# A fused attention and feed-forward kernel whose engine programs are written without a block

## The chip, the cores and the metric

The kernel runs on one core of a Trainium2 chip. The metric is the device time of one execution in microseconds (us); lower is better. Three executions of the kernel before gave 151.01, 150.97 and 151.39 us, a median of 151.01.

A core has five engines that run programs of their own: TensorE (PE, matrix products), VectorE (DVE), ScalarE (ACT), GpSimd (POOL) and SyncE (SP, which here issues nearly all transfers). They meet only through semaphores, counters that one engine or transfer raises and another waits for.

## The reference

The input x has 2048 tokens of 448 columns. It is normalised, and two branches are added to it: linear attention with 16 heads of 28 columns and softmax feature maps, and a feed-forward layer of width 1792 with the Mish activation.

```python
xn = _layernorm(x, axis=-1)
return x + _A_ref(xn, A_wqkv, A_w_phi, A_wo) + _B_ref(xn, B_w1, B_b1, B_w2)

# A: qkv = xn @ wqkv;  pq = q @ w_phi, pk = k @ w_phi (per head)
phi_q = concatenate([softmax(pq), softmax(-pq)]);  phi_k likewise
kv = einsum("bhsf,bhsd->bhfd", phi_k, v);  z = sum over s of phi_k
o = (phi_q @ kv) / (phi_q @ z + 1e-6)
A = o @ wo
# B: h = xn @ w1 + b1;  sp = log(1 + exp(h)), written stably
B = (h * tanh(sp)) @ w2
```

## The kernel before

The 2048 tokens are cut into 16 tiles of 128 (two tiles make a unit u, eight units). Loads of x and of the weights go out on SyncE's queue. VectorE, ScalarE and GpSimd normalise the tiles; the result is transposed and stays in on-chip memory. TensorE then works through keys, values and queries of all units (the helper at line 423 records most of these matmuls), the feed-forward layer's first product (line 423 as well, with the activation at line 699), the sums over tokens (line 649), the attention output (line 722), its product with wo (line 845) and the feed-forward layer's second product (line 828). The last two add up in the same accumulators. VectorE adds x (line 793) and SyncE stores two tiles at a time (line 859). The last tile, `LAST` = 15, is finished in two pieces: 384 columns, stored from ScalarE's queue, and 64 columns (lines 807 to 814), stored from SyncE's queue (both at line 856).

The order of the work is written out by hand: `ORDER` is a list of step names, and `run_order` calls them one by one. A step calls `op` or `dma` of the class `Program`, which only notes an instruction with its engine and what it reads and writes. `resolve` then works out which instructions must wait for which and gives them semaphores; each DMA has a semaphore of its own. Nothing reaches an engine until `emit(name, eng)` goes through one engine's list and writes its waits (line 131) and instructions in order.

After the last step one more instruction is noted, at line 928: an empty one on SyncE that reads every stored tile, and so waits for the landing of each store of the result:

```python
op("SP", lambda e: e.nop(), r=[("dram", t) for t in range(NT)] + [("draml", LAST)])
```

Then `resolve` runs and the five lists are emitted inside `with nc.Block() as block:` (line 931), each in a function of its own. When the `with` ends, the block is closed: every engine drains, and they meet at a barrier, in which GpSimd gathers a count from each engine and then lets all go. In the profile these instructions carry line 931. A similar meeting at the start of the program carries line 964, where the program object is made; it is not part of the kernel's function.

Of the kernel before, what the change touches and what calls it, by code (L numbers as in the profile page):

```python
# [5 lines left out]
ACT = mybir.ActivationFunctionType  # L6
# [132 lines left out]
def bass_parallel_sum__linear_kernel_hedgehog__dense_activation_mish__prompt_kernel(  # L139
    nc, A_x, A_wqkv, A_w_phi, A_wo, B_x, B_w1, B_b1, B_w2, out  # L140
):
    es = ExitStack()
    with es:
        _kernel(es, nc, A_x, A_wqkv, A_w_phi, A_wo, B_w1, B_b1, B_w2, out)
# [26 lines left out]
def _kernel(es, nc, A_x, A_wqkv, A_w_phi, A_wo, B_w1, B_b1, B_w2, out):  # L171
# [87 lines left out]
    pg = Program(nc, es)  # L259
# [668 lines left out]
    op("SP", lambda e: e.nop(), r=[("dram", t) for t in range(NT)] + [("draml", LAST)])  # L928

    pg.resolve()  # L930
    with nc.Block() as block:
        @block.sync
        def _(e):
            pg.emit("SP", e)

        @block.gpsimd
        def _(e):
            pg.emit("POOL", e)

        @block.tensor  # L940
        def _(e):
            pg.emit("PE", e)

        @block.scalar
        def _(e):
            pg.emit("ACT", e)

        @block.vector
        def _(e):
            pg.emit("DVE", e)  # L950


# [26 lines left out]
```

## Time and profile before

| | |
|---|---|
| median of three runs | 151.01 us |
| span of the profiled execution, first to last instruction | 148.7 us, 3864 instructions |
| median less span | 2.3 us |
| TensorE busy | 144.0 us, 97% of the span |
| VectorE, ScalarE, GpSimd busy | 102.7, 74.7 and 38.9 us |
| granted TensorE clock, mean | 1.000 |

The profile shows one execution and gives it no time but its span, which counts from the first instruction of the program to the end of the last. The timed runs are others, and hold besides what lies ahead of the program and behind it; no view shows that part. Times in the rows are counted from the span's start. Engine names that end in q (SPq, POOLq) mean the engine's sequencer: semaphore instructions, branches, drains and the issuing of DMAs, which are not counted as busy time. A row that begins with a line number groups the instructions which that line of the kernel made. The chain that ended last is found by going back from the last instruction through what released each step.

### The profile page before, as it was taken

The numbers are of one execution on the slowest core, as the hardware profiler recorded it, in microseconds if no ns is written. First come the engines' busy times: TensorE is split into PE (matmuls) and PEld (weight loads), VectorE is DVE, ScalarE is ACT, GpSimd is POOL, SyncE is SP. The second block draws the span as 40 slices with busy tenths as digits, with TensorE's granted clock in tenths as the row PEclk, the third lists the DMA queues.
The fourth block names the chain that finished last, engine by engine and source line by source line (L and its number), as shares of the span: only waits on it lengthen the run. The fifth ranks groups of instructions, "written<-read, shape, count | busy, mean of one in ns | idle before, by whom it ended". The sixth has DMA issues, their size and how long they took to land.

```text
span 148.7 us, 3864 instructions
## 1 busy us (share of the span) xinstructions
PE 144.0 (97%) x1669; PEld 74.2 (50%) x1669; DVE 102.7 (69%) x229; ACT 74.7 (50%) x91; POOL 38.9 (26%) x53
## 2 busy tenths in 40 slices
PE   6899999999999999999999999999999999999992
PEld 2365555555444555444444445545555555555561
DVE  0699898996999930407787989529983999930072
ACT  4997999779999999567747661002000000000000
POOL 4424465179999992000000000000000000000000
PEclk9999999999999999999999999999999999999999
DMA  4997997799699069499956053210013130551005
GB/s 131 245 278 216 119 185 149 126 170 344 103 188 196 14 52 132 85 239 295 195 98 125 4 62 62 43 23 0 7 37 86 35 93 0 123 127 58 4 10 175
DMA packets 39964, 17.23 MB, mean 116 GB/s; under 512 B 33932, under 2 KB 39180, under 8 KB 39948
## 3 DMA queue, kind: packets, MB, share of 16 engines
q1 hardware_dynamic: 39776, 16.89, 54.4%
q8 instruction: 13, 0.21, 0.6%
q10 hardware_dynamic: 172, 0.10, 0.2%
q14 instruction: 3, 0.02, 0.0%
HBM read 7.02 MB, written 1.84 MB: 60 GB/s over the span
## 4 chain that ended last, share of the span: by engine, by line
PE 92%; DMA 3%; DVE 2%; SPq 1%; issue 0%
PE PS L423 50%; PE PS L828 29%; PE PS L845 7%; DMA Wkv<-in_A_wqkv_dram 3%; PE PS L722 3%; PE PS L649 2%; PE PS L580 1%; DVE xn L497 1%; SPq L270 1%; PE PS L556 0%; PE PS L505 0%; DVE x_all L793 0%; DVE Eq L512 0%; DVE x_all L814 0%
## 5 line engine op out<-in xcount | busy, mean ns | idle before, releaser
L423 PE MATMUL PS<-xnT,W 64*128 64x512 bf16 x392 | 44.8, 377 | 0.0
L828 PE MATMUL PS<-W,actT 128*128 128x448 bf16 (+1 forms) x224 | 42.9, 351 | 0.0
L699 ACT ACTIVATE actT<-PS,b1T 128x1024 bf16<-128x1024 f32 x28 | 29.8, 1112 | 22.1 <-PE PS L423 22.1
L828 PEld LDWEIGHTS PS<-W,actT 128*128 128x128 bf16 x224 | 21.5, 98 | 19.8 <-issue 0.3
L423 PEld LDWEIGHTS PS<-xnT,W 64*128 64x128 bf16 x392 | 17.9, 94 | 21.9 <-PE PS L423 1.9
L630 POOL TENSOR_TENSOR actT<-actT,rSk 128x896 bf16<-128x896 bf16 x16 | 26.6, 1699 | 5.1 <-DVE rSk L628 5.1
L793 DVE TENSOR_TENSOR x_all<-PS,x_all 128x448 bf16<-128x448 f32 (+1 forms) x16 | 9.2, 613 | 15.2 <-PE PS L845 10.5
L626 DVE TENSOR_REDUCE Sk<-actT 128x32 f32<-128x896 bf16 x16 | 16.6, 1037 | 1.1 <-ACT actT L618 1.1
L618 ACT ACTIVATE actT<-PS 128x896 bf16<-128x896 f32 x16 | 13.7, 920 | 1.8 <-PE PS L423 1.7
L423 PE MATMUL PS<-Wpk,xnT 64*128 64x448 bf16 x112 | 13.2, 349 | 0.0
L423 PE MATMUL PS<-Wkv,xnT 64*128 64x448 bf16 x112 | 12.9, 349 | 0.0
L423 PE MATMUL PS<-Wpq,xnT 64*128 64x448 bf16 x112 | 12.6, 349 | 0.0
L738 DVE COPY Sq<-PS 128x16 f32<-128x16 f32 x32 | 4.0, 167 | 12.0 <-PE PS L722 12.0
L462 DVE BATCH_NORM_STATS2 stats<-x_all 128x6 f32<-128x448 bf16 x14 | 8.4, 601 | 3.4 <-DMA x_all<-in_A_x_dram 3.4
L746 DVE TENSOR_TENSOR v_all<-v_all 128x464 f32<-128x464 f32 x16 | 10.3, 641 | 0.6
L742 DVE TENSOR_TENSOR v_all<-PS,Sq 128x464 f32<-128x464 f32 x16 | 10.3, 641 | 0.5
L749 DVE TENSOR_TENSOR xn<-v_all,rden 128x448 bf16<-128x448 f32 x16 | 10.0, 625 | 0.6
L744 DVE TENSOR_TENSOR v_all<-PS,Sq 128x464 f32<-128x464 f32 x16 | 10.1, 629 | 0.0
L680 ACT ACTIVATE actT<-PS 128x896 bf16<-128x896 f32 x10 | 8.6, 930 | 0.1
L423 PEld LDWEIGHTS PS<-Wpq,xnT 64*128 64x128 bf16 x112 | 5.4, 94 | 5.0 <-ACT actT L680 0.2
L423 PEld LDWEIGHTS PS<-Wkv,xnT 64*128 64x128 bf16 x112 | 5.4, 94 | 5.1 <-ACT actT L618 0.2
L423 PEld LDWEIGHTS PS<-Wpk,xnT 64*128 64x128 bf16 x112 | 5.3, 94 | 5.1 <-issue 0.2
(83 smaller groups left out, 118.8 us busy)
## 6 DMA issues: line engine op xcount, KB each, us to landing
W<-in_B_w_dram SPq DMA_DIRECT2D x1, 1568.0 KB, 7.9
out_dram<-x_all SPq DMA_DIRECT2D x7, 224.0 KB, 2.2
W<-in_B_w_dram SPq DMA_DIRECT2D x1, 1344.0 KB, 7.0
x_all<-in_A_x_dram SPq DMA_DIRECT2D x4, 224.0 KB, 3.1
x_all<-in_A_x_dram SPq DMA_DIRECT2D x2, 448.0 KB, 4.9
Wkv<-in_A_wqkv_dram SPq DMA_DIRECT2D x2, 336.0 KB, 4.8
Wo<-in_A_wo_dram SPq DMA_DIRECT2D x2, 336.0 KB, 6.3
W<-in_B_w_dram SPq DMA_DIRECT2D x2, 224.0 KB, 4.1
```

The source lines that it names most:

```text
L423: ins = e.matmul(o, lhs(c, k), rhs(c, k), start=first and n == at[par][0], stop=last and n == at[par][-1])
L618: op("ACT", lambda e, s=s: e.activation(E_of(u)[:, s, :, :], two(b, D), ACT.Exp, scale=1.0 if s == 0 else -1.0), r=[pb(b), pb(b + 1)], w=[ ...
L626: op("DVE", lambda e: e.tensor_reduce(Sk[u][:, s, :], Eh(), AX.X, ALU.add), r=[("E", u, s)], w=[("Sk", u, s)], tag=f"Sk{u}.{s}")
L630: op("POOL", lambda e: e.tensor_tensor(Eh(), Eh(), ap_on(rSk[u][:, s, 0:1], [[1, 2 * H], [0, DH]]), ALU.mult), r=[("E", u, s), ("rSk", u, ...
L699: op("ACT", lambda e: e.activation(actT[:, fc, q * 1024:(q + 1) * 1024], bank(b, 2), ACT.Mish, bias=b1T[:, fc:fc + 1]), r=[("b1T",), pb(b) ...
L742: op("DVE", lambda e: e.tensor_tensor(tv(t1[i]), num(0), sx(1), ALU.mult), r=[pb(b), pb(b + 1), ("Sq", i, 1)], w=[("t1", i)], tag=f"ta{t}")
L744: op("DVE", lambda e: e.tensor_tensor(tv(t2), num(1), sx(0), ALU.mult), r=[pb(b), pb(b + 1), ("Sq", i, 0)], w=[("t2",)], tag=f"tb{t}")
L746: op("DVE", lambda e: e.tensor_tensor(t1[i], t1[i], t2, ALU.add), r=[("t1", i), ("t2",)], w=[("t1", i)], tag=f"tc{t}")
L749: op("DVE", lambda e: e.tensor_tensor(o_sb[(t // 2) % 2][:, t % 2, :].rearrange("p (h d) -> p h d", d=DH), t1[i][:, :, 0:DH], ap_on(rden[i ...
L793: op("DVE", lambda e: e.tensor_tensor(x_all[:, t, 0:n], bank(b)[:, 0:n], x_all[:, t, 0:n], ALU.add), r=[pb(b), ("x", t)], w=[("out", t)], ...
L828: ins = e.matmul(bank(b)[:, 0:width(t)], actT[:, fc, tok(t)], W2[:, fc, 0:width(t)], start=first and fc == 0, stop=last and fc == FC - 1)
L845: ins = e.matmul(bank(b)[:, 0:w], oT_of(u)[lo:hi, cc * P:(cc + 1) * P], Wo[lo:hi, cc, 0:w], start=first and n == at[par][0], stop=last and ...
```

## The change

The five lists are emitted straight to the five engines, one after the other, with no block around them. The lists themselves, their order, their semaphores and SyncE's last instruction, which waits for every store, are as they were. With the block go the branches into and out of it and the closing barrier: nothing that the kernel writes makes TensorE, ScalarE, VectorE or GpSimd wait for the stores any more.

```diff
     pg.resolve()
-    with nc.Block() as block:
-        @block.sync
-        def _(e):
-            pg.emit("SP", e)
-
-        @block.gpsimd
-        def _(e):
-            pg.emit("POOL", e)
-
-        @block.tensor
-        def _(e):
-            pg.emit("PE", e)
-
-        @block.scalar
-        def _(e):
-            pg.emit("ACT", e)
-
-        @block.vector
-        def _(e):
-            pg.emit("DVE", e)
+    for name, eng in (("SP", nc.sync), ("POOL", nc.gpsimd), ("PE", nc.tensor), ("ACT", nc.scalar), ("DVE", nc.vector)):
+        pg.emit(name, eng)
```

## The prediction

> **What bounds the kernel now.** I read the page first, then the chain of waits, then the end of the timeline with the DMA issues, and last the instructions of line 931, where the block opens and, on exit, its closing code is recorded.
>
> ```profile
> span 148.7 us, 3864 instructions
> ...
> PE 144.0 (97%) x1669; PEld 74.2 (50%) x1669; DVE 102.7 (69%) x229; ACT 74.7 (50%) x91; POOL 38.9 (26%) x53
> ...
> PE 92%; DMA 3%; DVE 2%; SPq 1%; issue 0%
> ```
>
> TensorE holds 92% of the chain that ended last. The change touches none of its matmuls, so for nearly all of the span the question is only whether the same instructions run at the same pace. What can differ stands at the two edges. The last steps of the chain of waits, and the last two issues of the timeline with the rows of the same transfers among the DMA issues (size, then us from issue to landing):
>
> ```profile
> 142.98 2.42 PE PS L828 x14
> 145.40 0.02 issue
> 145.42 0.56 DVE x_all L793
> 145.98 0.19 DVE x_all L814
> ```
>
> ```profile
> 146.01 0.38 ACTq L856 DMA_DIRECT2D out_dram<-x_all  x1
> 146.20 0.33 SPq L856 DMA_DIRECT2D out_dram<-x_all  x1
> ```
>
> ```profile
> out_dram<-x_all ACTq DMA_DIRECT2D x1, 96.0 KB, 1.7
> ...
> out_dram<-x_all SPq DMA_DIRECT2D x1, 16.0 KB, 1.7
> ```
>
> TensorE's last group starts at 142.98, VectorE's last addition ends at 145.98 + 0.19 = 146.17, and the last store goes out at 146.20 and lands 1.7 us later, at 147.9. So the last 2.5 us of the span (146.2 to 148.7) hold no computing: 1.7 us are the store's flight, and the rest, 148.7 - 147.9 = 0.8 us, comes after everything is in memory. The next rows show what that rest is. They are the instructions of line 931 (engine, operation, count, least/median/greatest duration in ns, start of the first and the last), then SyncE's wait for the stores at line 928, and SyncE's own row of waits.
>
> ```profile
> L931 POOLq EVENT_SEMAPHORE  x2: 17/17/17, 148.2 to 148.6; - x2
> L931 POOLq DRAIN  x1: 319/319/319, 75.4 to 75.4; - x1
> L931 PEldq DRAIN  x1: 715/715/715, 145.2 to 145.2; - x1
> L931 DVEq DRAIN  x1: 264/264/264, 146.0 to 146.0; - x1
> L931 ACTq DRAIN  x1: 143/143/143, 146.4 to 146.4; - x1
> L931 SPq COMPARE_BRANCH  x1: 33/33/33, 148.0 to 148.0; - x1
> L931 SPq DRAIN  x1: 13/13/13, 148.1 to 148.1; - x1
> L931 SPq EVENT_SEMAPHORE  x1: 17/17/17, 148.6 to 148.6; - x1
> L931 ACTq EVENT_SEMAPHORE  x1: 17/17/17, 148.6 to 148.6; - x1
> L931 DVEq EVENT_SEMAPHORE  x1: 21/21/21, 148.6 to 148.6; - x1
> L931 PEldq EVENT_SEMAPHORE  x1: 51/51/51, 148.6 to 148.6; - x1
> ```
>
> ```profile
> L928 SPq EVENT_SEMAPHORE  x1: 28/28/28, 147.9 to 147.9; - x1
> ```
>
> ```profile
> SPq L928 <- DMA out_dram<-x_all: 1.1, 1, 1.1
> ...
> SPq L931 <- PEq L931: 0.5, 1, 0.5
> ```
>
> The reader is to see a barrier with SyncE as the last to arrive. Four engines have drained by 146.4 + 0.14 = 146.6. SyncE has waited 1.1 us for the stores, goes on at 147.9, branches at 148.0, drains at 148.1. GpSimd gathers the five arrivals at 148.2, lets them go only at 148.6, and the last release, TensorE's 51 ns, closes the span at 148.7. Of this, SyncE's 0.5 us wait is all spent on the barrier.
>
> **The change part by part.** Twelve instructions carry line 931: one branch, five drains, six semaphore instructions. All twelve go.
>
> *Drains of the four engines that have finished.* GpSimd's 319 ns at 75.4, TensorE's 715 ns at 145.2, VectorE's 264 ns at 146.0 and ScalarE's 143 ns at 146.4 gain nothing by themselves: all are over by 146.6, under SyncE's wait that lasts to 147.9. Without that cover the latest, ScalarE's, would be worth its 0.14 us.
>
> *SyncE's branch and drain, GpSimd's gather and release, the four other releases.* These stand one after the other behind the last store, with nothing beside them. SyncE's last store wait is the branch's own place: the branch starts at 148.0 and takes 33 ns, and since line 928's wait ended just before, the kernel's last instruction in the changed program, a wait or an empty instruction on the last store, should take the branch's place and its length. I count its end as 148.0. What goes is 148.7 - 148.0 = 0.7 us; the starts are rounded to 0.1, so 0.6 to 0.8. By parts: branch to drain 0.1, drain to gather 0.1, gather to release 0.4, release to the last engine's end 0.1.
>
> *Entry.* The words of the change speak of branches into the block. Line 931 lists a single branch, SyncE's on the way out. At the start there stands a barrier of line 964, which is made with the program and stays; its rows, and what follows in the timeline:
>
> ```profile
> L964 POOLq EVENT_SEMAPHORE  x2: 17/17/17, 0.6 to 0.7; - x2
> ...
> L964 SPq EVENT_SEMAPHORE  x1: 17/17/17, 0.7 to 0.7; - x1
> L964 ACTq EVENT_SEMAPHORE  x1: 17/17/17, 0.7 to 0.7; - x1
> ```
>
> ```profile
> 0.80 0.53 POOL L339 MEMSET v_all<- 128x256 uint32 x1 [0.29 <-POOLq L964]
> 0.80 0.87 SPq L270 DMA_DIRECT2D x_all<-in_A_x_dram  x2
> 0.80 1.28 ACT L310 ACT_TABLE_LOAD   x1 [0.80 <-PEq L964]
> ```
>
> Three engines begin their own work at 0.80, at most 0.1 us after their release at 0.7. A branch that left no record has 0 to 0.1 us there; I take 0, since a step from one instruction to the next has to fit into the same gap. The same instructions then follow in the same order on every queue. Should the build, seeing one run of code per engine, place one more table load on ScalarE at the start, it costs ScalarE 1.28 us, and this wait hides it:
>
> ```profile
> ACT junk L453 <- DMA x_all<-in_A_x_dram: 1.3, 1, 1.3
> ```
>
> Beyond that cover it would delay the first statistics, and then the first chain step that needs them; I put it at 0.
>
> [...]
>
> *Around the span.* The profiled execution has a span of 148.7; the timed runs have a median of 151.01, so 151.01 - 148.7 = 2.3 us are not in any view (work around the program, and whatever a profiled execution differs by). Work after the span now starts on all engines at one moment, 148.7. After the change SyncE reaches it at 148.0, the others at 146.6 or before, GpSimd at 75.4 + 0.3 = 75.7. If that work waits for all five engines first, the time shifts with SyncE alone: -0.7. Bounds: if it asks GpSimd for a reply of the slow kind again (0.4 at the end against 0.1 from gather to release at the start), 0.3 of the gain goes, leaving -0.4, and all of it, 0, if the end needs the whole exchange again. On the other side, if its longest part belongs to an engine other than SyncE, that part starts up to 148.7 - 146.6 = 2.1 us sooner. I take -0.7, nearest to the rows that are on the path.
>
> Sum: against the profile, 148.7 - 0.7 = 148.0; against the median, 151.01 - 0.7 = **150.3 us** (0.5% less).
>
> **The rivals.**
>
> *More is gained (B).* The runtime's closing work of the four early engines slips under the store's flight of 1.7 us. For it: they are idle from 146.6. Against it: a closing sequence that resets anything must wait for SyncE. Time: the bound of 2.1 taken half, about 1.1, gives 149.9; range 148.9 to 150.2.
>
> *Less is gained (C).* GpSimd's slow release returns in the closing work. For it: the same pair of instructions took 0.1 at the start, 0.4 after GpSimd had been idle since 75.7, so the delay may belong to the idle engine, not to the barrier. Against: that work had its own exchanges within the 2.3 us already. Time 151.01 - 0.4 = 150.6; down to no gain, 151.0. [...]
>
> *The change doesn't do what it says (D).* The build closes a program without a block with a barrier of its own: 151.0. Nothing speaks for it but that the opening barrier of line 964 is also made without the kernel's asking.
>
> [...]
>
> **How the numbers follow.** A, the forecast, 150.3 (150.15 to 150.45): 0.52. B 0.17, C 0.17 (half at 150.6, half close to 151.0), D 0.07, E and anything like it 0.07. The range reaches from the middle of B, 149.7, to no gain, 151.0, and leaves out about 0.07 at either end. A measurement of this kernel can tell about 0.3%, 0.45 us, from no change, so faster means below 150.56: A and B, and a little of C, together 0.71; same: the rest of C, and D, 0.22; slower 0.07.
>
> **What would show it.** In the changed kernel's profile no row of line 931's kind should stand at the end; the last instruction should be SyncE's wait for the stores, at 147.9 to 148.0, and the span should be 148.0 with some 12 instructions fewer. The first DMA should still stand at 0.80, the last store at 146.2 with 1.7 us to landing, "issue" at 0%. A span of 148.0 with a median above 150.6 is C; a median under 150.1 with that span is B; a new barrier behind 148.0 is D; TensorE's last group starting later than 142.98 by more than a few tenths, with idle time before it put down to "issue", is E. The prediction is wrong outright if the span stays at 148.7, or if the time falls by more than the store's whole flight.

## The result and the profile after

The changed kernel takes 149.47 us (median of six executions, 149.18 to 149.91) against 150.99 us of the kernel before (six, 150.87 to 151.39). The ratio is 0.989, with a 95% interval of 0.9867 to 0.9913, so 0.9% to 1.3% less, about 1.5 us. The forecast was 150.3 us with a range of 149.7 to 151.0: the direction was right, the size half of what was measured, and the time lies below the range. All figures are of undisturbed executions.

The page of the changed kernel opens with these rows:

```profile
span 148.1 us, 3852 instructions
...
PE 93%; DMA 2%; DVE 1%; ACT 1%; POOL 1%; issue 0%
```

Twelve instructions fewer, as counted. The end of the chain of waits, the last two issues of the timeline, and the same two transfers among the DMA issues:

```profile
143.09 2.42 PE PS L828 x14
145.53 0.56 DVE x_all L793
```

```profile
146.12 0.39 ACTq L856 DMA_DIRECT2D out_dram<-x_all  x1
146.31 0.33 SPq L856 DMA_DIRECT2D out_dram<-x_all  x1
```

```profile
out_dram<-x_all ACTq DMA_DIRECT2D x1, 96.0 KB, 1.7
out_dram<-x_all SPq DMA_DIRECT2D x1, 16.0 KB, 1.7
```

Each stands 0.11 us later than in the profile of before, with the same flight of 1.7 us: the work itself isn't quicker. Then SyncE's own waits and the one row of its last instruction:

```profile
SPq L928 <- DMA out_dram<-x_all: 0.9, 1, 0.9
```

```profile
L928 SPq EVENT_SEMAPHORE  x1: 168/168/168, 147.9 to 147.9; - x1
```

Nothing of line 931's kind is left. The program ends with SyncE's wait, at 147.9 + 0.17 = 148.1. At the other edge the timeline is as it was, within 0.01 us (line 946 is here what line 964 was):

```profile
0.80 0.53 POOL L339 MEMSET v_all<- 128x256 uint32 x1 [0.29 <-POOLq L946]
0.80 0.39 SPq L270 DMA_DIRECT2D x_all<-in_A_x_dram  x1
0.81 1.28 ACT L310 ACT_TABLE_LOAD   x1 [0.81 <-PEq L946]
```

So the profile shows what was forecast for it: 148.7 to 148.1, 0.6 us. The time fell by 1.5. The question for the experiments was where the other 0.9 us came from.

One number has to be put right first. For every later execution both time and span are known, and the span of the profile of before turned out to be a short one. The kernel before, in 29 executions on one chip, has spans of 148.6 to 149.7 (median 149.1), and its time less its span is 2.05 us on average (1.99 to 2.11). The changed kernel has spans of 147.7 to 148.8 and a time less span of 1.25 us in each of three groups of six. The drop of 1.5 to 1.6 us is thus 0.75 to 0.8 in the span and 0.8 behind or ahead of it.

### The profile page after: what moved, and what is told of

It reads as the page before. It is cut to its first block, busy times and chain, and to the rows that moved or that the text cites. A ratio compares the mean times of both kernels' runs of the same rounds, so it can differ in the third digit from the quotient of the medians.

```text
span 148.1 us, 3852 instructions
## 1 busy us (share of the span) xinstructions
PE 143.2 (97%) x1669; PEld 75.3 (51%) x1669; DVE 102.8 (69%) x229; ACT 74.5 (50%) x91; POOL 38.7 (26%) x53
## 4 chain that ended last, share of the span: by engine, by line
PE 93%; DMA 2%; DVE 1%; ACT 1%; POOL 1%; issue 0%
PE PS L423 51%; PE PS L828 29%; PE PS L845 7%; PE PS L722 3%; DMA x_all<-in_A_x_dram 2%; PE PS L649 2%; PE PS L580 1%; DVE xn L497 1%; PE PS L505 1%; ACT junk L458 1%; POOL rstd L473 0%; ACT junk L453 0%; DVE x_all L793 0%; PE PS L556 0%; POOL lnv L470 0%
## 5 line engine op out<-in xcount | busy, mean ns | idle before, releaser
L423 PEld LDWEIGHTS PS<-xnT,W 64*128 64x128 bf16 x392 | 18.4, 94 | 21.5 <-PE PS L423 1.9
```

The lines of the kernel that those rows point to most:

```text
L423: ins = e.matmul(o, lhs(c, k), rhs(c, k), start=first and n == at[par][0], stop=last and n == at[par][-1])
```

## The experiments

The following table has all kernels that were run. The ratio is to the kernel before on the same chip, with its interval; "less span" is the mean of time less span. The rows of block_only and pe_waits_stores rest on three executions, those of the other changed kernels on four to twelve.

| kernel | time, us | ratio | span, us | less span, us |
|---|---|---|---|---|
| before (four chips) | 150.99 to 151.34 | 1 | 148.95 to 149.3 | 2.03 to 2.05 |
| changed | 149.47 | 0.989 (0.9867 to 0.9913) | 148.25 | 1.25 |
| barrier_back | 150.77 | 0.9966 (0.9949 to 0.9984) | 148.95 | 1.85 |
| all_wait_stores | 150.80 | 0.9952 (0.9938 to 0.9966) | 148.7 | 2.12 |
| pe_waits_stores | 149.83 | 0.990 (0.9884 to 0.9917) | 148.1 | 1.73 |
| dve_waits_stores | 149.79 | 0.9895 (0.988 to 0.991) | 148.4 | 1.36 |
| before_again | 151.38 | 1.0012 (0.9991 to 1.0033) | 149.35 | 2.05 |
| after_again | 149.62 | 0.9893 (0.9864 to 0.9922) | 148.35 | 1.25 |
| pool_waits_stores | 150.42 | 0.9958 (0.994 to 0.9975) | 148.3 | 2.12 |
| pool_awake_block | 150.88 | 0.9987 (0.9968 to 1.0005) | 148.9 | 1.99 |
| block_only | 149.84 | 0.9918 (0.9891 to 0.9946) | 148.5 | 1.34 |
| three_wait_stores | 149.96 | 0.9929 (0.9908 to 0.995) | 148.2 | 1.75 |
| no_opening_barrier | 149.60 | 0.9902 (0.9882 to 0.9923) | 147.8 | 1.70 |
| after_third | 149.86 | 0.9912 (0.9888 to 0.9936) | 148.6 | 1.25 |
| pool_awake_waits | 150.34 | 0.9957 (0.9924 to 0.9989) | 148.05 | 2.28 |
| two_barriers | 151.24 | 1.0004 (0.9989 to 1.0019) | 149.1 | 2.07 |

The span moves by up to 1.7 us from execution to execution of one kernel (before_again, 148.5 to 150.2); "less span" by about 0.1 in most kernels, by 0.2 in two_barriers and by 0.5 in no_opening_barrier (1.44 to 1.92). The second is therefore the sharper measure of what happens around the program.

### Barrier or block

The barrier is put behind the changed kernel, without a block:

```diff
         pg.emit(name, eng)
+    nc.all_engine_barrier()
```

> No block, but one barrier of all five engines after the last emitted instruction. Theory (the gain comes from the barrier: 0.6 us inside the span, the rest because four engines now reach the work behind the program early): both parts go, span about 148.6 to 148.7, time 150.8 to 151.0, time less span 2.3. Rival (the branches and the layout of blocks are worth something of their own): the barrier's 0.6 us come back in the span, but time less span stays near 1.25, so time about 150.1.

The time rose to 150.77: two thirds of the gain are gone, in the span and in "less span" alike. The profile of this kernel has the old rows again, less the branch (here line 933):

```profile
L933 POOLq EVENT_SEMAPHORE  x2: 17/17/17, 148.7 to 149.1; - x2
...
L933 SPq DRAIN  x1: 13/13/13, 148.6 to 148.6; - x1
...
L933 PEldq EVENT_SEMAPHORE  x1: 51/51/51, 149.1 to 149.1; - x1
```

From SyncE's drain to the last release are 149.1 - 148.6 = 0.5 us, and GpSimd again takes 0.4 from gather to release. But 0.57 us are still missing to the 151.34 of before on that chip (the interval says 0.24 to 0.77). So the block has a price of its own when there is a barrier behind it. The converse is a block with its branches, whose closing barrier is taken out of the program:

```diff
             pg.emit("DVE", e)
+    closing = nc.cur_bb.bb
+    closing.instructions = [i for i in closing.instructions if type(i).__name__ not in ("InstDrain", "InstEventSemaphore")]
```

> The block with its branches into and out of it, but the five engines' closing barrier is taken out of the program. Theory (barrier and block add up: barrier 0.6 in the span and 0.6 behind it, branches 0.2 in the span and 0.2 outside it): span 148.5 to 148.6, time less span 1.45, time 149.9 to 150.0. Rival (what putting the barrier back left over, 0.2 in time less span, was chance): time as the changed kernel, 149.5 to 149.6, less span 1.25.

Its ratio, 0.9918, can't be told from the changed kernel's on the same chip, 0.9912, and "less span" is 1.34 against 1.25. The theory had 1.45, the rival 1.25; it lies between. The barrier is worth 0.6 in "less span" with no block around (1.85 to 1.25), and 0.7 with one (2.04 to 1.34); the block 0.1 to 0.2.

### Who is late at the end

Behind the span there is no row of the program, but the trace keeps when a semaphore is changed. One that this kernel doesn't use, number 2, is changed nine times about the program's end (in the kernel before, all nine from 148.94 to 149.52, behind the span's end at 148.70) and nine times again from about 0.8 us after the ninth; each change is called a raise below. Between the two nines stands a long row of other semaphores, 236 in the kernel before (149.46 to 150.09) and 237 in the changed one (148.29 to 148.93), each changed once. The moments, in us from the span's start:

```
                     span's end  first meeting: 5 going up                  4 coming back                second ends
before               148.70      148.94 148.97 149.24 149.28 149.31   149.40 149.44 149.48 149.52   150.67
changed              148.05      146.20 146.77 146.81 146.85 148.17   148.22 148.26 148.29 148.34   149.51
dve_waits_stores     148.45      146.58 147.16 147.20 148.59 148.62   148.71 148.75 148.79 148.83   150.01
pool_waits_stores    148.09      146.22 146.80 148.96 149.00 149.03   149.12 149.16 149.20 149.24   150.39
pe_waits_stores      147.98      148.18 148.21 148.25 148.29 148.32   148.41 148.69 148.72 148.77   149.93
three_wait_stores    148.53      148.75 148.78 148.82 148.87 148.89   148.99 149.28 149.31 149.36   150.49
all_wait_stores      149.11      149.30 149.33 149.99 150.03 150.06   150.15 150.19 150.23 150.27   151.41
barrier_back         149.17      149.41 149.45 149.71 149.76 149.78   149.88 149.92 149.95 150.00   151.15
```

Which engine is late decides how many raises are early, so the rows are read here as a meeting of the five engines in one order. In the changed kernel four hand-offs are done by 146.85, long before the last store lands at 148.03, and the fifth, at 148.17, follows SyncE's end at 148.05. With VectorE late three are early (to 147.16), with GpSimd late two (to 146.80), with TensorE late none (the first at 148.18): in these runs the order is TensorE, ScalarE, GpSimd, VectorE, SyncE (ScalarE's place is the one left over), and then back, by the seventh raise (below) in reverse. From the span's end to the meeting's end are 149.52 - 148.70 = 0.83 us before and 148.34 - 148.05 = 0.28 after; from there to the last hand-off of the second meeting 1.15 and 1.17, so nothing changes there. With all engines waiting for the stores (all_wait_stores) the first of these stretches takes 150.27 - 149.11 = 1.16. Whoever comes early has done its part.

These moments hold 0.54 us of the 0.80 that "less span" fell. Where one execution has its time and its moments on record, its time is 0.18 us less than the moment of the second end in the changed kernel (149.65 against 149.83 in after_again) and in the kernels that only add waits to it, but 0.06 us more in before_again (151.40 against 151.34) and 0.15 less in barrier_back. So another 0.24 us of the gain lie ahead of the span or behind the second end; what they are no record tells, and 0.21 of them are gone as soon as the block is, even with the barrier kept.

These kernels make one engine or all four wait for the last two stores, as SyncE does:

```diff
     op("SP", lambda e: e.nop(), r=[("dram", t) for t in range(NT)] + [("draml", LAST)])
+    for eng in ("POOL", "PE", "ACT", "DVE"):
+        op(eng, lambda e: e.nop(), r=[("dram", LAST), ("draml", LAST)])
```

(all_wait_stores; the others have ("PE",), ("DVE",), ("POOL",), or all but GpSimd.)

> No block and no barrier, but TensorE, ScalarE, VectorE and GpSimd each end with a wait of their own for the last tile's two stores, as SyncE does. Theory (what is gained behind the span is gained by the four engines' early arrival): span stays at about 148.1, time less span goes back to about 2.3, time about 150.4. Rival (time less span fell because the barrier's own instructions are gone, not because anybody is early): time less span stays at 1.25, time 149.5.

> As the changed kernel, but TensorE alone ends with a wait for the last two stores. Theory (the work behind the program begins with a chain of hand-offs from engine to engine that starts at TensorE and ends at SyncE, 0.4 us long): with TensorE late the whole chain has to run after the stores, span 148.1, time 150.0 to 150.4. Rival (only the number of late engines counts, or only SyncE): time 149.5 to 149.7.

> As the changed kernel, but VectorE alone ends with a wait for the last two stores. Theory (a chain in which VectorE stands right before SyncE): one hand-off of under 0.1 us is added, time 149.5 to 149.6, span 148.1. Rival (any engine that is late costs the same): as with TensorE alone, 150.0 to 150.4.

> As the changed kernel, but GpSimd alone ends with a wait for the last two stores. Theory (GpSimd's sequencer, idle since 76, needs 0.3 to 0.6 us more for its first step after it wakes, and in the changed kernel this falls under the stores' flight): span 148.1 to 148.4, time less span 1.6 to 1.9, time 150.0 to 150.4. Rival (the slow release belonged to the barrier's own code): as with VectorE alone, time less span 1.3 to 1.4, time 149.7.

> As the changed kernel, but TensorE, ScalarE and VectorE each end with a wait for the last two stores; GpSimd does not. Theory (a chain from TensorE to SyncE and back, with GpSimd slow only after it wakes): as with TensorE alone, time less span 1.73, time 150.0. Rival (three late engines add up, and GpSimd plays no part of its own): time less span 2.1, as with all four, time 150.4.

All four late: less span 2.12, as the theory had it, though there is no barrier; its span stays low. The rows of that kernel's waits:

```profile
L930 ACTq EVENT_SEMAPHORE  x1: 171/171/171, 148.9 to 148.9; - x1
L930 POOLq EVENT_SEMAPHORE  x1: 171/171/171, 148.9 to 148.9; - x1
L930 DVEq EVENT_SEMAPHORE  x1: 173/173/173, 148.9 to 148.9; - x1
L930 PEldq EVENT_SEMAPHORE  x1: 171/171/171, 148.9 to 148.9; - x1
```

Everybody is let go at one moment, 148.9, by the store itself; no drain, no gather, no release stands behind it, and 0.87 us (2.12 - 1.25) are lost all the same. So what the change gains in the closing meeting is early arrival and not the barrier's instructions. With one engine late: VectorE 1.36 (+0.11), TensorE 1.73 (+0.48), GpSimd 2.12 (+0.87). Three without GpSimd give 1.75, the same as TensorE alone; GpSimd alone gives the same as all four. Lateness doesn't add up: what counts is the engine from which the rest of the order has still to be gone through, and GpSimd has a price of its own.

That price shows on the way back too. The seventh raise, GpSimd's if the way back is the order reversed, follows the sixth by 0.28 us in pe_waits_stores and 0.29 in three_wait_stores, and by 0.04 in the other rows of the table. In these two GpSimd's hand-off on the way up, its first step after some 70 us, came only 0.44 and 0.46 us earlier; between gather and release in the kernel's own barrier it was 0.41. So about half of TensorE's 0.48 is GpSimd's slow reply, and in the changed kernel, where 1.45 us lie between its two steps, it is hidden.

### Why GpSimd is dear

The table of moments shows it: late alone, GpSimd needs from its program's end 148.96 - 148.09 = 0.87 us to its hand-off, VectorE 0.15, TensorE 0.19, SyncE 0.12. In the kernel before, its hand-off comes 0.27 us after ScalarE's, where the changed kernel has 0.04. Whether this is its waking from 70 us of idleness was tried with three kernels. In the first, with block and barrier, GpSimd fills two columns after VectorE's last addition:

```diff
+    op("POOL", lambda e: e.memset(mhalf[:], -0.5), r=[("outl", LAST)], w=[("mhalf",)], tag="awake")
```

> The kernel before with its block and barrier; only GpSimd ends with a two-column fill that waits for VectorE's last addition, so it wakes at 146.2 and not at 148.2. Theory (the slow step is the first after waking): the barrier's release follows the gather after 0.1 and not 0.4 us, span and time 0.3 less, 150.7 to 151.0 against 151.0 to 151.3. Rival (the slow release belongs to the barrier's code): span and time as before.

The second has that line and then, without block and barrier, GpSimd's wait for the stores:

> As the changed kernel with GpSimd alone waiting for the last two stores, but GpSimd first does a two-column fill that waits for VectorE's last addition, so it has been awake for some 2 us when the stores land. Theory (what makes GpSimd dear is its first step after some 70 us of idleness): time less span falls from 2.12 to about 1.5, time 149.7 to 149.9. Rival (GpSimd is slow after any wait that it ends with, idle before or not): time less span 2.1, time 150.4.

The third has the line `nc.all_engine_barrier()` twice:

> No block, and two barriers of all engines one after the other at the end. Theory (GpSimd's release is late in the first barrier alone, for it has just been woken): the second barrier adds 0.25 to the span, time less span stays near 1.85, time 151.0. Rival (every barrier has the late release): the second adds 0.55 to 0.6, time 151.3.

Gather and release of GpSimd in pool_awake_block, line 932, and in the first and second barrier of two_barriers, lines 933 and 934 (start of the first and of the last of the two):

```profile
L932 POOLq EVENT_SEMAPHORE  x2: 17/17/17, 149.0 to 149.1; - x2
```

```profile
L933 POOLq EVENT_SEMAPHORE  x2: 17/17/17, 148.5 to 148.9; - x2
```

```profile
L934 POOLq EVENT_SEMAPHORE  x2: 17/17/17, 149.2 to 149.3; - x2
```

0.1 us where it was awake, 0.4 where it had been idle, 0.1 in a second barrier right behind. The slow release inside the barrier goes with its having been idle. In times this is little: pool_awake_block is at 0.9987 with an interval across 1, so the 0.3 us that the rows show can't be told from nothing there; and two_barriers came out at 151.24, nearer to the rival's 151.3, as its span grew, measured against before on each chip, by the 0.3 us of the second barrier's rows, but its less span also rose, from 1.85 to 2.07, which nothing here explains.

The wait before the closing meeting is another matter. pool_awake_waits has less span 2.28, no better than 2.12, and its hand-off comes 1.03 us after its program's end: here the theory is wrong. GpSimd needs 0.6 us (in the kernel before, 148.6 to 149.24) to 1.0 us (here) between its program and its hand-off in the kernels above in which it is late, woken before or not. What it does in that time isn't in the trace, and stays open.

### The same two kernels again, and the other edge

> The kernel before, unchanged, to see its time and its span in the same executions. Theory (the profiled execution shown of before was a quick one, and its real time less span is nearer to 2.0 than the 2.3 worked out from a median of other executions): time less span 2.0, spans 149.1 to 149.5. Rival (2.3 is right, and the gain behind the span is 1.05): 2.3.

> The changed kernel, unchanged, beside the kernel before on one chip. Theory: time less span 1.25 again, span some 1.0 below that of before, of which the barrier is 0.56 and SyncE's branch 0.1 to 0.2; so the last store lands about 0.3 sooner than before. Rival (no part of the work itself is quicker, the earlier spans differed by chance): the last store lands as late as before, the time gains 1.2 to 1.3 and not 1.5.

> The changed kernel, unchanged, on the chip of these runs, for comparison. Both theories: time less span 1.25, time 149.4 to 149.7.

Time less span was 2.05 and 1.25 as the theory had it. In the profiled executions of the two, the last store landed at 148.57 (before) and 148.38 (changed), 0.19 sooner; in the first pair it landed at 147.90 and 148.03, 0.13 later. Both differences are well within what the span moves by. From the landing to the span's end are 0.80 and 0.02 us; this 0.78 is about the 0.75 between the median spans, 149.1 (29 executions) and 148.35. So nothing shows that the work itself became quicker, which is the rival's view, and the rest of the gain is outside the span. The rival's gain of 1.2 to 1.3 us is at the low end of the interval (1.2 to 2.1), though; the medians are 1.49 apart.

As the closing barrier cost more than its own rows, the opening one was taken out as well:

```diff
+    entry = nc.cur_bb.bb
+    entry.instructions = [i for i in entry.instructions if type(i).__name__ not in ("InstDrain", "InstEventSemaphore")]
     for name, eng in (("SP", nc.sync), ("POOL", nc.gpsimd), ("PE", nc.tensor), ("ACT", nc.scalar), ("DVE", nc.vector)):
```

> The changed kernel without the barrier at the start of the program either, which comes with the program object and not with the kernel; the constants that it guards are read by nothing here. Theory (a barrier that every engine reaches at once costs its exchange alone, and the first loads of x wait behind it): loads start 0.5 to 0.7 us sooner after the program's start, time 0.4 to 0.7 below the changed kernel, 148.9 to 149.2. Rival (the loads are bound by what precedes the program, or the time's start moves along): time as the changed kernel, 149.5 to 149.6.

Its first rows, from the timeline:

```profile
0.00 0.87 SPq L270 DMA_DIRECT2D x_all<-in_A_x_dram  x2
0.12 1.28 ACT L310 ACT_TABLE_LOAD   x1
```

The loads start at 0.00 and not at 0.80, and the span falls by 0.8; but less span rises by 0.45 (1.25 to 1.70), and the ratio, 0.9902, can't be told from the 0.9912 of the changed kernel beside it. The time came out as the rival had it, and the theory's 148.9 to 149.2 was missed. The loads do go out sooner: the meeting ahead of the program, read from the same semaphore, ends at -0.01 here and at 0.00 in the changed kernel, so the span is counted from the same moment. About 0.14 us of what is lost again stand between the first and the second end behind the program (1.30 us against 1.15 to 1.17); where the rest is lost the trace doesn't show. No version was found that is surely quicker than the changed kernel.

## Why the prediction was wrong in size

*Drains of the four early engines, nothing.* Right: with the barrier back and the drains with it, the last of the four (ScalarE's, at 147.1 for 0.14 us) ends under SyncE's wait for the landing at 148.56.

*SyncE's branch and drain, gather, release: 0.7 us.* Right. 148.7 to 148.1 in the two profiles shown, 0.75 between medians on one chip, 0.78 between landing and end in the second pair of profiles.

*Entry, nothing.* Right as to the rows: the first three starts are at 0.80 before and at 0.80 to 0.81 after. The block alone, without a barrier, can't be told from no block.

*Around the span, nothing.* This is the term that failed. The step reasoned that work behind the program which waits for all five engines shifts with SyncE alone. By the moments it does wait for all five, but in one order in which SyncE comes last, so four of the five hand-offs on its way up are done under the stores' flight when the others come early (146.85 against 148.03 in the changed kernel). That is rival B's mechanism, and the prediction's own sign for B, a span of 148.0 with a median under 150.1, came true. The taken value was 0; measured is -0.8 (2.05 to 1.25). By the runs, -0.6 of it is the barrier's and -0.1 to -0.2 the block's; by the moments, -0.54 is the shorter closing meeting, and -0.24 has no mechanism shown. The forecast's own bound for it, up to 2.1 us more, had room for this. B's 149.9 was nearer than the forecast, but by luck: no row gave the half of the bound that it took. It was put at 0.17. The range began at 149.7, which the prediction calls B's middle; the middle of B's own bounds, 148.9 to 150.2, is 149.55. The step also spoke against B that a closing sequence must wait for SyncE. In the changed kernel only its last hand-off and the way back came behind SyncE (148.17 to 148.34).

The 2.3 us for "around the span" joined a median with a profile of other executions. Read in one execution it is 2.05.

*C, GpSimd's slow reply returns.* Its premise holds in part: in the barrier the reply is slow after idleness. It was taken as a loss, yet it is a reason for more gain: in the changed kernel GpSimd's program is over at 76, and the 0.6 to 1.0 us that it needs before its hand-off are hidden. The slow reply itself returns behind the span only in pe_waits_stores and three_wait_stores (0.28 and 0.29 us), where GpSimd's first step after its idleness stands in the closing meeting and the reply is due within 0.2 us.

*D, a barrier of the build's own.* No: there is no such row. *E, slower, given 0.07.* No run shows the delay that it stands for. In its place the runs showed "issue" at 0% of the chain, before and after, and a last TensorE group that starts 0.11 us later (143.09 against 142.98) than in a profile whose span was among the shortest.

## What to carry to other kernels

In this kernel a barrier at the very end costs more than its rows: 0.6 us in the span and as much again behind it, because it makes all engines late for the closing meeting (0.83 us from the span's end against 0.28) that they could have begun while the last store was under way. Let only one engine wait for the stores, the one that the closing order needs last (here SyncE: less span 1.25, against 1.73 with TensorE waiting too and 2.12 with GpSimd), and let GpSimd finish early. And take the time and the span from the same execution before working out what lies around the span. No other kernel was run.

## What the runs showed that had not been expected

GpSimd alone, late at the end, costs as much as all four engines late (less span 2.12 in both, against 1.25), VectorE only 0.11. Waking GpSimd 2 us before doesn't help it (2.28), though inside a barrier it does (0.1 against 0.4 us from gather to release). How the 0.2 us arise that a block adds to less span in front of a barrier (2.04 against 1.85), and the 0.2 that a second barrier adds, was not settled; the first isn't in the closing meeting, which takes 0.83 us in both.
